# Two of six batches of triangular systems solved by halves of 16 rows and joined by matrix products

## The chip, the cores and the metric

One core of one Trainium2 chip runs the whole program. The metric is the device time of one execution in microseconds (us), the median of several runs. The engines are TensorE (PE, its weight loads shown apart as PEld), VectorE (DVE), ScalarE (ACT), GpSimd (POOL), and SyncE (SP), which issues most of the transfers. They work side by side and wait for each other by semaphores.

## The reference

The program is a recurrent attention over 768 steps for 4 x 8 heads of 40 features, followed by two feed-forward blocks on the 3072 tokens:

```python
for t in range(S):
    y[:, :, t] = np.einsum('bhd,bhde->bhe', rt, state)
    Sa = np.einsum('bhde,bhe->bhd', state, at)
    state_decay = state * wt[:, :, None, :] - np.einsum('bhd,bhe->bhde', Sa, bt)
    state = state_decay + np.einsum('bhd,bhe->bhde', vt, kt)
...
h = np.maximum(np.maximum(x @ w1, x @ w2), x @ w3); x = h @ w_out
h = x @ w_in; sp = np.log1p(np.exp(h)); x = (h * np.tanh(sp)) @ w_out2
```

The steps are cut into chunks of 32. Inside a chunk, the effect of its own steps on each other is a lower triangular system of 32 rows for each head and chunk: with A the products of a and b below the diagonal, the chunk needs the inverse of a unit triangular matrix, which is computed once and then applied by a matrix product.

## The kernel before

**Chunks, units, batches.** The 32 heads go in two groups of 16 through 24 chunks each, so there are 48 chunks, `c` = 0 to 47. Two chunks that follow each other are a unit `n` (24 of them), and four units are a batch `k` (six of them). A unit holds 8 systems in each of four groups of 32 partitions (`zo`); a batch holds 32 "items" in each group, so 128 systems of 32 x 32.

**`pre(n)`** prepares a unit: a scan over the decays (L240), the decayed a, b and k (L244 to L265), and then the `m1` products (L275), which go through a PSUM buffer with the tag `un` that has a single copy. From it ACT copies the triangular part to `ab` (L280), which is one buffer for the whole batch, and VectorE transposes the other part (L282), which GpSimd masks into `ax` (L288).

**`solve(k)`** transposes `ab` so that the 128 systems of the batch lie one in each partition (L303), and eliminates row by row: for s = 0 to 30 a multiply into `tv` (L308) and a subtract from T (L310), both on VectorE, over all rows below s and columns up to s. T then holds the inverse (with sign), is transposed back into `tr[k % 2]` (L314), squared on ACT for a check of its size (L315), and cleared on GpSimd for the next batch (`clear`, L294 and L295).

**`chain(c)`** is the serial work of a chunk in five stages: x0 (L386), its product with the inverse `ups` (L400, weights from `tr`, 16 matmuls of 32 x 32 tiles, four row groups at work), a transpose (L411), the score products (L353, masked at L423), and the output and the next state (L436, L441, L443). `kb` (L325, L329) transposes k and b of the next unit through the same `un` buffer.

**The order.** `start` does units 0 to 3, the solve of batch 0 and the loads of the first chunks. `run` then goes through the chunks in five slots each. A slot issues a stage of the chain; then `fill`, which brings the conversions of the feed-forward weights (L587 to L651) and, from chunk 5 on, eight matmuls of the first feed-forward block (`group`, L661 to L665, L771, L812) a slot; then one step of `pre` for up to three or four units ahead; then some steps of the next solve, spread so that it ends when the chunk that needs it begins; then the rest of the chain's stage; then `kb`, if `un` is not held (`self.held`). The solve of batch 1 can start when units 4 to 7 are prepared, which comes in chunk 4, and must end before chunk 8.

TensorE and VectorE run each of these two blocks (`start`; `run`) in program order, ACT too in `start` and from chunk 4 on. Between the blocks, and on the other engines and queues, a planner puts the instructions in order from simulated times. VectorE's and TensorE's queues are in order, so an instruction that waits holds all that stands behind it.

The second feed-forward block (L941 to L990) runs after the chunks and ends the program.

Of the kernel before, what the change touches and what calls it, by code (L numbers as in the profile page):

```python
# [17 lines left out]
C = 32  # L18
# [74 lines left out]
EARLY = 37  # L93
NPOOL = 14
NE = 3
IN_ORDER = {mybir.EngineType.PE, mybir.EngineType.DVE}


# [55 lines left out]
class Attention:  # L154
# [78 lines left out]
    def pre(self, n):  # L233
# [31 lines left out]
        nc.vector.tensor_tensor(out=bv[:, 8:16], in0=bv[:, 8:16], in1=Qv[:, 8:16], op=ALU.mult)  # L265
        if n >= NB:
            yield
        ps = self.ps_un.tile([128, 2, 4, 64], F32, name="m1", tag="un")
        self.held = True
        for cc in range(2):  # L270
# [10 lines left out]
        akT = p1.tile([128, 4, 2, C], F32, name="akT")  # L281
        nc.vector.transpose(out=akT.rearrange("p j c t -> p c j t"), in_=ps[:, :, :, 0:C])  # L282
        self.held = False
        yield
        for zo in range(4):
            y, g = 1 - zo // 2, zo % 2
# [9 lines left out]

    def solve(self, k):

        nc, p1 = self.nc, self.p1
        abT, T = self.tr[k % 2], self.T  # L300
        if k == 0:
            self.clear()
        nc.vector.transpose(out=abT, in_=self.ab.rearrange("p i s -> p s i"))  # L303
        yield
        for s in range(C - 1):
            n = C - 1 - s
            tv = p1.tile([128, 256], F32, name="tv")[:, 0:n * (s + 1)].rearrange("p (t j) -> p t j", t=n)
            nc.vector.tensor_tensor(out=tv, in0=abT[:, s, s + 1:C].unsqueeze(2).to_broadcast([128, n, s + 1]),  # L308
                                    in1=T[:, s, 0:s + 1].unsqueeze(1).to_broadcast([128, n, s + 1]), op=ALU.mult)
            nc.vector.tensor_tensor(out=T[:, s + 1:C, 0:s + 1], in0=T[:, s + 1:C, 0:s + 1], in1=tv, op=ALU.subtract)  # L310
            yield
        yield

        nc.vector.transpose(out=self.tr[k % 2], in_=T)  # L314
        nc.scalar.activation(out=T, in_=T, func=AF.Square, accum_out=self.gate.le(1e4))  # L315
        if k + 1 < len(self.last):
            self.clear()
        yield
# [144 lines left out]

    def start(self):
        nc, A = self.nc, self.A
        self.under, self.next, self.done, self.held = [], 0, 0, False

        def zeros(*ts):
            for t in ts:
# [45 lines left out]
    def run(self, fill):  # L515
# [6 lines left out]
        for c in range(NC):  # L522
# [4 lines left out]
            for slot in range(5):  # L527
# [12 lines left out]
                if left <= 0 and k + 1 < len(self.last) and self.done > self.last[k + 1] and \  # L540
                        (k == 0 or (c, slot) >= (2 * self.last[k - 1] + 1, 2)):
                    k += 1
                    solve = self.solve(k)
                    left = 34
                    due = 2 * (self.last[k - 1] + 1)
                if left > 0:
                    steps = -(-left // max(1, 5 * (due - c) - slot - 1))
# [725 lines left out]
```

## Time and profile before

| what | us |
|---|---|
| median of 3 runs | 1072.44 |
| lowest and highest run | 1069.83, 1076.19 |
| span of the profiled execution, first to last instruction | 1070.9 |
| TensorE busy | 912.0 (85%) |
| VectorE busy | 878.3 (82%) |
| ScalarE busy | 731.2 (68%) |
| GpSimd busy | 339.6 (32%) |

The profile is of one execution. Its only time of its own is the span, which lies within the spread of the runs; durations below are read from it. Busy shares are means over stages that have different bounds, so the stage in which the change acts has to be looked at by itself. In timelines a group such as x32 is 32 instructions that ran one behind the other and stand in one row, and the time in brackets is how long the engine sat idle before it, with what ended the wait. Matmul instructions overlap each other, so the duration of one is longer than the distance between the starts of two.

### The profile page before, as it was taken

What the parts mean: (1) busy time and instruction counts of PE and PEld (TensorE: products, weight loads), DVE (VectorE), ACT (ScalarE), POOL (GpSimd) and SP (SyncE); (2) the same over time, 40 slices, a digit from 0 to 9 for tenths busy, and PEclk for the clock granted to TensorE, in tenths of its full rate; (3) what the DMA queues carried; (4) which work ended last, traced back from release to release, by engine and by line L of the source; (5) the groups of instructions that cost most, each with busy time, mean ns of one, the idle gap of its engine ahead of it and who ended that gap; (6) DMA issues with size and microseconds to landing.
All of it is one profiled execution on the core that took longest, in us unless ns stands there. A gap on an engine that the chain in (4) does not pass through costs nothing.

```text
span 1070.9 us, 34069 instructions
## 1 busy us (share of the span) xinstructions
PE 912.0 (85%) x14098; PEld 816.2 (76%) x14098; DVE 878.3 (82%) x1698; ACT 731.2 (68%) x1886; POOL 339.6 (32%) x422
## 2 busy tenths in 40 slices
PE   1313456899999999999999999979999999999996
PEld 1212345888888888888998888878889998888995
DVE  7589979978968987886688666899988989898875
ACT  4638864465566665656667777677787887878874
POOL 7437894333233242323114334681201002010000
PEclk9999999999999999999999999999999999999999
DMA  8415532243433434333334443530100000010000
GB/s 211 134 62 159 144 91 64 71 128 84 114 101 100 110 96 113 94 88 97 81 85 104 132 134 90 173 108 5 30 25 31 25 30 26 1 54 1 25 1 28
DMA packets 110615, 87.03 MB, mean 81 GB/s; under 512 B 72740, under 2 KB 89764, under 8 KB 110452
## 3 DMA queue, kind: packets, MB, share of 16 engines
q1 hardware_dynamic: 109712, 84.54, 29.0%
q8 instruction: 113, 1.85, 0.8%
q14 instruction: 50, 0.41, 0.1%
q10 hardware_dynamic: 740, 0.23, 0.1%
HBM read 72.16 MB, written 12.58 MB: 79 GB/s over the span
## 4 chain that ended last, share of the span: by engine, by line
PE 56%; DVE 23%; ACT 9%; issue 4%; DMA 4%; POOL 2%; SPq 0%; ACTq 0%; DVEq 0%; POOLq 0%
PE cops L988 5%; PE cops L989 5%; PE cops L990 5%; PE ys L436 4%; PE bps L661 4%; PE cps L661 4%; PE cps L662 4%; PE cps L663 4%; PE bps L812 3%; DVE T L310 3%; PE bps L662 3%; PE bps L663 3%; DVE tv L308 3%; PE cgps L353 2%; PE cps L665 2%
## 5 line engine op out<-in xcount | busy, mean ns | idle before, releaser
L661 PE MATMUL bps<-bxh,bw 128*128 128x256 f32 x432 | 139.9, 325 | 2.3 <-DVE mx L771 1.4
L662 PE MATMUL bps<-bxl,bw 128*128 128x256 f32 x432 | 124.1, 287 | 3.2 <-DVE bxl L674 3.2
L663 PE MATMUL bps<-bxh,bw 128*128 128x256 f32 x432 | 122.8, 284 | 0.0
L774 POOL TENSOR_TENSOR hl<-mx,hh 128x256 fp32r<-128x256 f32 x72 | 56.7, 787 | 172.8 <-ACT hh L773 145.2
L310 DVE TENSOR_TENSOR T<-T,tv 128x31 f32<-128x31 f32 (+15 forms) x186 | 86.4, 464 | 6.4
L661 PEld LDWEIGHTS bps<-bxh,bw 128*128 128x128 f32 x432 | 82.5, 191 | 11.4 <-DVE mx L771 2.0
L252 POOL TENSOR_TENSOR ax<-ax,pp 40x256 f32<-40x256 f32 x96 | 75.4, 805 | 45.1 <-DMA ax<-in_A_dram 16.1
L662 PEld LDWEIGHTS bps<-bxl,bw 128*128 128x128 f32 x432 | 83.2, 193 | 5.4 <-DVE bxl L674 5.4
L288 POOL TENSOR_SCALAR_AFFINE_SELECT ax<-akT 32x256 f32<-32x256 f32 x96 | 51.3, 535 | 104.6 <-DVE akT L282 100.6
L663 PEld LDWEIGHTS bps<-bxh,bw 128*128 128x128 f32 x432 | 83.1, 192 | 0.0
L972 ACT ACTIVATE e<-e 128x512 f32<-128x512 f32 x93 | 58.6, 630 | 33.3 <-DVE e L970 33.0
L436 PE MATMUL ys<-rs,ls 128*40 128x72 f32 x1536 | 64.8, 241 | 14.6 <-DVE rs L423 9.9
L812 PE MATMUL bps<-hh,bo 128*128 128x256 f32 x360 | 74.9, 291 | 1.5 <-ACT mx L769 1.5
L984 DVE TENSOR_TENSOR gl<-e,gh 128x512 fp32r<-128x512 f32 x93 | 65.8, 708 | 12.5 <-ACT gh L983 12.5
L976 DVE SCALAR_TENSOR_TENSOR e<-e,r 128x512 f32<-128x512 f32 x93 | 66.0, 710 | 11.7 <-ACT r L974 11.4
L275 PE MATMUL m<-bk,ax 40*32 40x64 f32 x1536 | 43.1, 254 | 38.1 <-DMA bk<-in_KB_dram 14.6
L436 PEld LDWEIGHTS ys<-rs,ls 128*40 128x40 f32 x1536 | 55.6, 126 | 22.0 <-DVE rs L423 9.4
L441 DVE TENSOR_TENSOR sv<-ys,pp 40x320 f32<-40x320 f32 x92 | 44.7, 486 | 32.1 <-PE ys L436 31.4
L941 POOL CAST cxh<-cxl 128x1536 fp32r<-128x1536 f32 x5 | 9.1, 1814 | 193.8 <-DMA cxl<-x 193.8
L771 DVE TENSOR_TENSOR mx<-bps,mx 128x256 f32<-128x256 f32 x144 | 60.3, 419 | 11.6 <-ACT mx L769 7.7
L977 DVE SCALAR_TENSOR_TENSOR e<-e,r 128x512 f32<-128x512 f32 x93 | 68.2, 734 | 1.0
L308 DVE TENSOR_TENSOR tv<-tr,T 128x31 f32<-128x31 f32 (+15 forms) x186 | 67.1, 361 | 1.9
(214 smaller groups left out, 3108.3 us busy)
## 6 DMA issues: line engine op xcount, KB each, us to landing
bk<-in_KB_dram SPq DMA_DIRECT2D x24, 448.0 KB
sv<-in_SV_dram SPq DMA_DIRECT2D x96, 80.0 KB
raw<-in_w_dram SPq DMA_DIRECT2D x18, 384.0 KB
w<-in_W_dram SPq DMA_DIRECT2D x21, 231.0 KB
v<-in_VT_dram SPq DMA_DIRECT2D x48, 96.0 KB
rs<-in_RT_dram SPq DMA_DIRECT2D x48, 96.0 KB
cxl<-x SPq DMA_DIRECT2D x12, 384.0 KB
raw<-in_wo_dram SPq DMA_DIRECT2D x13, 320.0 KB
```

The costliest lines, as they stand in the source:

```text
L252: nc.gpsimd.tensor_tensor(out=xv[:, h], in0=xv[:, h], in1=P[ro, h, 0:C], op=ALU.mult)
L308: nc.vector.tensor_tensor(out=tv, in0=abT[:, s, s + 1:C].unsqueeze(2).to_broadcast([128, n, s + 1]), in1=T[:, s, 0:s + 1].unsqueeze(1).to_ ...
L310: nc.vector.tensor_tensor(out=T[:, s + 1:C, 0:s + 1], in0=T[:, s + 1:C, 0:s + 1], in1=tv, op=ALU.subtract)
L436: nc.tensor.matmul(out=self.ys[64 * y:64 * y + 40, p, 0:72], lhsT=l[:, y, p], rhs=r_[:, :, 4 * (p % 4) + 2 * (1 - y) + p // 4], start=True ...
L661: nc.tensor.matmul(out=ps, lhsT=h[:, k], rhs=xh[:, k], start=(k == 0), stop=False)
L662: nc.tensor.matmul(out=ps, lhsT=h[:, k], rhs=xl[:, k], start=False, stop=False)
L663: nc.tensor.matmul(out=ps, lhsT=l[:, k], rhs=xh[:, k], start=False, stop=False)
L771: after(1, lambda ps=ps, mx=mx: nc.vector.tensor_tensor(out=mx, in0=ps, in1=mx, op=ALU.max))
L812: nc.tensor.matmul(out=pss[d][rows], lhsT=lhsT, rhs=rhs, start=first, stop=last)
L976: nc.vector.scalar_tensor_tensor(out=e, in0=e, scalar=1.0, in1=r, op0=ALU.add, op1=ALU.mult)
L977: nc.vector.scalar_tensor_tensor(out=e, in0=e, scalar=-float(np.sqrt(8.0)), in1=r, op0=ALU.add, op1=ALU.mult)
L984: nc.vector.tensor_tensor(out=gl, in0=e, in1=gh.bitcast(F32), op=ALU.subtract)
```

## The change

`HALVED = 2`: batches 0 and 1 are solved by `solve_halves`, the other four as before (`solve_whole` is the old `solve`). The two diagonal blocks of 16 rows of each system are eliminated in the same VectorE operations, 15 steps instead of 31; an access pattern with a step of (C + 1) * H elements covers both. T is then transposed into `tr` as before and, new, also in place. `join` fills the lower left block: a product of `ab` with the second half's inverse (64 matmuls, for 16 items in four row groups), a copy by ACT, a product with the first half's inverse (64 matmuls), and an add by VectorE into `tr`. It runs twice, for items 0 to 15 and 16 to 31, and both times through the `un` buffer. The square for the check reads `tr` and comes behind the joins, and the clearing of T behind that.

Since the join reads `ab` again, `pre` may not write it before: from the start of a halved solve to its second join (`self.joins`), units wait ahead of their `m1` products, and afterwards pass there in their order (`self.turn`). The steps over which `run` spreads the solve are 20 instead of 34 for these batches.

```diff
@@ -265,6 +266,8 @@
         nc.vector.tensor_tensor(out=bv[:, 8:16], in0=bv[:, 8:16], in1=Qv[:, 8:16], op=ALU.mult)
         if n >= NB:
             yield
+        while self.joins or self.turn < n:
+            yield
         ps = self.ps_un.tile([128, 2, 4, 64], F32, name="m1", tag="un")
         self.held = True
         for cc in range(2):
@@ -281,6 +284,7 @@
         akT = p1.tile([128, 4, 2, C], F32, name="akT")
         nc.vector.transpose(out=akT.rearrange("p j c t -> p c j t"), in_=ps[:, :, :, 0:C])
         self.held = False
+        self.turn = n + 1
         yield
         for zo in range(4):
             y, g = 1 - zo // 2, zo % 2
@@ -296,10 +300,73 @@
 
     def solve(self, k):
 
+        if k < HALVED:
+            return self.solve_halves(k)
+        return self.solve_whole(k)
+
+    def join(self, k, h):
+
+        nc, T, tt = self.nc, self.T, self.tr[k % 2].rearrange("p t i -> p i t")
+        ps = self.ps_un.tile([128, 2, 16, 16], F32, name="join", tag="un")
+        items = range(16 * h, 16 * h + 16)
+        for i in items:
+            for zo in range(4):
+                zr = slice(32 * zo, 32 * zo + 32)
+                nc.tensor.matmul(out=ps[zr, 0, i % 16], lhsT=self.ab[zr, i], rhs=tt[zr, i, 16:32], start=True, stop=True)
+        e = self.p1.tile([128, 256], F32, name="tv").rearrange("p (i t) -> p i t", t=16)
+        nc.scalar.copy(out=e, in_=ps[:, 0])
+        yield
+        for i in items:
+            for zo in range(4):
+                zr = slice(32 * zo, 32 * zo + 32)
+                nc.tensor.matmul(out=ps[zr, 1, i % 16], lhsT=T[32 * zo:32 * zo + 16, i], rhs=e[32 * zo:32 * zo + 16, i % 16],
+                                 start=True, stop=True)
+        low = tt[:, 16 * h:16 * h + 16, 16:32]
+        nc.vector.tensor_tensor(out=low, in0=low, in1=ps[:, 1], op=ALU.add)
+
+    def solve_halves(self, k):
+
         nc, p1 = self.nc, self.p1
         abT, T = self.tr[k % 2], self.T
+        H = C // 2
+
+        def halves(x, t, n, j, m):
+            x = x[:, t, j:j + 1]
+            return bass.AP(x.tensor, x.offset, [x.ap[0], [(C + 1) * H, 2], n, m])
+
         if k == 0:
             self.clear()
+        self.joins = True
+        nc.vector.transpose(out=abT, in_=self.ab.rearrange("p i s -> p s i"))
+        yield
+        for s in range(H - 1):
+            n = H - 1 - s
+            tv = p1.tile([128, 256], F32, name="tv")[:, 0:2 * n * (s + 1)].rearrange("p (h t j) -> p h t j", h=2, t=n)
+            nc.vector.tensor_tensor(out=tv, in0=halves(abT, s, [1, n], s + 1, [0, s + 1]),
+                                    in1=halves(T, s, [0, n], 0, [1, s + 1]), op=ALU.mult)
+            to = halves(T, s + 1, [C, n], 0, [1, s + 1])
+            nc.vector.tensor_tensor(out=to, in0=to, in1=tv, op=ALU.subtract)
+            yield
+        nc.vector.transpose(out=self.tr[k % 2], in_=T)
+        tn = T.rearrange("p t j -> p j t")
+        nc.vector.transpose(out=tn, in_=tn)
+        for h in range(2):
+            while self.held:
+                yield
+            self.held = True
+            yield from self.join(k, h)
+            self.held = False
+            self.joins = h == 0
+            yield
+        nc.scalar.activation(out=T, in_=self.tr[k % 2], func=AF.Square, accum_out=self.gate.le(1e4))
+        if k + 1 < len(self.last):
+            self.clear()
+        yield
+
+    def solve_whole(self, k):
+
+        nc, p1 = self.nc, self.p1
+        abT, T = self.tr[k % 2], self.T
         nc.vector.transpose(out=abT, in_=self.ab.rearrange("p i s -> p s i"))
         yield
         for s in range(C - 1):
@@ -463,7 +530,7 @@
 
     def start(self):
         nc, A = self.nc, self.A
-        self.under, self.next, self.done, self.held = [], 0, 0, False
+        self.under, self.next, self.done, self.held, self.joins, self.turn = [], 0, 0, False, False, 0
 
         def zeros(*ts):
             for t in ts:
@@ -541,7 +608,7 @@
                         (k == 0 or (c, slot) >= (2 * self.last[k - 1] + 1, 2)):
                     k += 1
                     solve = self.solve(k)
-                    left = 34
+                    left = 20 if k < HALVED else 34
                     due = 2 * (self.last[k - 1] + 1)
                 if left > 0:
                     steps = -(-left // max(1, 5 * (due - c) - slot - 1))
```

## Rows read from the trace of the kernel before

**Rows 1.** The page: span, and busy tenths of 40 equal slices.
```profile
span 1070.9 us, 34069 instructions
...
PE   1313456899999999999999999979999999999996
...
DVE  7589979978968987886688666899988989898875
```

**Rows 2.** Stretches: length; busy PE, PEld, DVE, ACT, POOL; granted clock; DMA share; GB/s.
```profile
106.00:160.00 54.00, 25.66 (x648) 20.89 (x648) 45.45 (x67) 40.45 (x133) 47.46 (x58) 1.00 0.44 121
...
330.00:690.00 360.00, 346.18 (x7321) 314.17 (x7309) 277.50 (x638) 236.55 (x754) 121.07 (x164) 1.00 0.41 108
```

**Rows 3.** Timeline of VectorE, batch 0's solve: start us, duration us, instruction.
```profile
42.59 0.19 DVE L308 TENSOR_TENSOR tv<-tr,T 128x31 f32<-128x31 f32 x1
...
43.06 0.22 DVE L308 TENSOR_TENSOR tv<-tr,T 128x60 f32<-128x60 f32 x1
...
43.58 0.25 DVE L308 TENSOR_TENSOR tv<-tr,T 128x87 f32<-128x87 f32 x1
...
44.15 0.27 DVE L308 TENSOR_TENSOR tv<-tr,T 128x112 f32<-128x112 f32 x1
...
67.50 1.25 DVE L314 STREAM_TRANSPOSE tr<-T 128x1024 f32<-128x1024 f32 x1
```

**Rows 4.** Timeline of TensorE, small products; in brackets idle before, and releaser.
```profile
23.72 1.92 PE L275 MATMUL m<-bk,ax 40*32 40x64 f32 x60 [0.30 <-DVE bk L265]
...
68.79 0.76 PE L400 MATMUL ups<-X,tr 32*32 32x40 f32 x32 [20.11 <-DVE tr L314]
...
221.12 0.67 PE L400 MATMUL ups<-X,tr 32*32 32x40 f32 x32
221.72 0.39 PE L812 MATMUL bps<-hl,bo 128*128 128x256 f32 x1
```

**Rows 5.** Chain of waits after the solve: start us, us, what.
```profile
68.83 1.16 ACT T L315 x2
...
70.10 1.07 POOL T L294
...
71.56 1.31 POOL t L597
```

**Rows 6.** Groups by line, 0 to 190 us: busy us, mean ns, idle before.
```profile
L303 DVE STREAM_TRANSPOSE tr<-ab 128x1024 f32<-128x1024 f32 x2 | 3.8, 1924 | 0.0
...
L280 ACT COPY ab<-m 128x256 f32<-128x256 f32 x10 | 3.7, 368 | 2.2 <-PE m L275 2.0
...
L443 DVE TENSOR_TENSOR YT<-ys,pp 104x256 f32<-104x256 f32 x5 | 2.1, 426 | 0.2
```

**Rows 7.** Instructions on the tile ups: ns min/median/max, first and last start.
```profile
L400 PE MATMUL ups<-X,tr x1536: 222/223/276, 68.8 to 662.3; 32*32 32x40 f32 x192
```

**Rows 8.** Stretches of batch 1's solve, columns as in rows 2.
```profile
161.20:172.20 11.00, 7.22 (x203) 5.98 (x203) 10.54 (x24) 4.76 (x13) 4.90 (x7) 1.00 0.40 110
172.20:178.00 5.80, 5.39 (x51) 4.75 (x52) 5.59 (x12) 2.48 (x9) 2.35 (x4) 1.00 0.30 58
178.00:187.20 9.20, 4.80 (x148) 4.11 (x147) 8.00 (x17) 4.15 (x11) 3.74 (x5) 0.91 0.05 12
187.20:198.60 11.40, 9.92 (x141) 8.87 (x142) 9.88 (x22) 4.17 (x14) 3.63 (x5) 0.77 0.42 107
198.60:222.00 23.40, 21.43 (x502) 19.13 (x502) 22.18 (x51) 13.97 (x42) 8.05 (x14) 1.00 0.26 65
```

**Rows 9.** Timeline of TensorE, chunk 5.
```profile
187.22 0.96 PE L325 MATMUL kb<-cst,bk 104*128 104x104 f32 x4 [4.42 <-DVE akT L282]
```

**Rows 10.** A stretch behind that gap, columns as in rows 2.
```profile
188.00:190.00 2.00, 2.00 (x34) 1.89 (x32) 1.66 (x4) 1.32 (x5) 1.85 (x4) 0.50 0.43 66
```

**Rows 11.** Chain of waits, one 256-column product behind the gap and later.
```profile
190.77 0.21 PE bps L662
...
201.27 0.12 PE bps L662
```

More of the change, by code (lines that the diff above doesn't have):

```diff
@@ L95 @@
 NE = 3
+HALVED = 2
 IN_ORDER = {mybir.EngineType.PE, mybir.EngineType.DVE}
```

## The prediction

> **What bounds the kernel now.** I read the page's tenths by slice first, then the busy time by stretch, then the timelines of the two stretches in which the first two batches are solved, and the chain that ended last between them. The reader is to see three regimes. Up to about 190 us TensorE is 10 to 70% busy and VectorE, but for one slice, 70% and more [rows 1]. From about 215 us on TensorE is the bound: in the stretch from 330 to 690 us it is busy 346.2 of 360 us, 96%, VectorE 77% [rows 2]. What is won in the first regime moves the start of the second, and what is added to TensorE after it adds to the end. Both edits must be priced so: batch 0 is solved alone, in the first regime; batch 1 is solved during chunks 4 to 7, where one regime passes into the other.
>
> Batch 0: from the first multiply at 42.59 us to the transpose of T at 67.50 VectorE runs nothing but the 62 operations of the solve, and TensorE's first `ups` product waits for that transpose until 68.79 us, having idled 20.1 us [rows 3, 4]. The chain that ended last runs through the same place and on through the clearing of T on GpSimd to the first weight conversion there [rows 5]. So a microsecond saved here is a microsecond of everything behind it.
>
> **Batch 0, part by part.** The distance from one operation's start to the next grows with the elements of one: two of 31 take 42.59 to 43.06, 0.235 us each, two of 87 take 0.285 each [rows 3], so 0.00089 us an element. The halved solve has 15 steps of two operations, of 2(s+1)(15-s) elements: 30, 56, 78, 96, 110, 120, 126, 128 and back. The first seven come to 0.235 + 0.257 + 0.277 + 0.293 + 0.305 + 0.314 + 0.320 = 2.00 us; twice that and 0.32 for the middle one, times two operations, is 8.65 us. The transpose into `tr` stays at 1.25 us [rows 3]; with 0.04 to the next start, 1.29.
>
> New is the in-place transpose of T, with strided input and output. The nearest row is L303, strided input alone, 1.92 us [rows 6]; it can't be under the 1.25 of contiguous data, nor do I see over 2.6 (strided twice). It lies beside the first product of the join, which needs only `tr`, and costs nothing while that product and its copy (below: 2.55 us) last longer.
>
> New are two joins, one behind the other, since each takes the one PSUM buffer `un`. Each is a 64-matmul product, an ACT copy of 256 columns (0.37 us as L280), a second 64-matmul product, and a VectorE add of 256 columns from PSUM (0.43 us as L443) [rows 6]. A float32 matmul is two instructions here: the 16 of `ups` are x32 [rows 4]. So a product is 128. `ups` has the same 32x32 tiles; its 32 instructions take 0.76 us at the start of the kernel and 0.67 later, one lasting 0.26 and 0.22 [rows 4, 7], so a distance of 16 and 14.4 ns. A join's matmul moves 16 columns instead of 40, which can only help, but reads them in steps of 128 bytes. Upper bound: the 60 of L275 in 1.92 us at the start, (1.92 - 0.3)/59 = 27 ns [rows 4]; lower bound, by the columns alone, 16/40 of 16, 6 ns. I take 15 ns (nearest row: the same tile shape). A product is then 1.92 + 0.25 = 2.17 us, a join 2 x 2.17 + 0.37 + 0.43 + four handovers of 0.05 = 5.3, both 10.7 us.
>
> Sum: 8.65 + 1.29 + 10.7 = 20.6 us against 26.2 (42.59 to 68.79): **5.6 us earlier**. Were `ups` of chunk 0, which reads only items of the first half, let in behind the first join and the second's first product, another 3.1 us (5.3 less 2.17) would be won; the order is the planner's, so I keep this as a bound. Bounds for batch 0: from +0.5 (27 ns: 2 x 8.4 + 9.9 - 26.2) to -9. The square and the clearing of T move behind the last join; the first weight conversion on GpSimd stands behind that clearing, 70.10 then 71.56 [rows 5], and moves with it.
>
> **Batch 1.** Removed on VectorE are the same 32 operations and three quarters of the elements. In the trace the stretch from 161 to 222 us has VectorE busy 10.5 of 11.0, 5.6 of 5.8, 8.0 of 9.2, 9.9 of 11.4 and 22.2 of 23.4 us [rows 8]. From 172.2 us (first feed-forward products) to 222 TensorE works 41.5 of 49.8 us, so 8.3 idle; at the later regime's 3.8% it would be 1.9: **6.4 us to win**. Most of it is one gap: 4.4 us before 187.22, in which `kb` waits for VectorE [rows 9], busy 8.0 of 9.2 us there [rows 8], much of it solve steps; of these, one in two is gone. Behind that gap the granted clock is 0.50, so 1.2 of 2.4 GHz, and the same product takes 0.21 us where it takes 0.12 later [rows 10, 11]; the mean of 187.2 to 198.6 is 0.77 [rows 8], so 0.46 of 11.4 us, 5.2, lie at that level, and half of them, **2.6**, goes with the gap. In chunk 4 (161.2 to 172.2), TensorE idles 3.8 us beside a full VectorE; the steps in it shrink by about 2 us: **2.0**.
>
> Against this stand four products, 512 instructions, in chunk 7, where TensorE is 92% busy [rows 8]: 512 x 14.4 ns is 7.4, and each change of shape costs what `ups` costs beyond its own instructions (0.60 us to the next start, 221.12 to 221.72, less 32 x 14.4 ns: 0.14), 0.6: **8.0 us added**. Moved are the `m1` products of units 8 to 11: they write `ab`, which the join reads, so `pre` holds them from the start of solve 1 until its second join, counted out on the code's slots at chunk 7, slot 3; then they follow each other within ten slots, through the same PSUM buffer. Their number is unchanged. What queues behind them: TensorE, in order, waits at each handover for the ACT copy and the VectorE transpose of the one before; a slot's feed-forward matmuls stand between (eight, of which one takes 0.12 to 0.21 us [rows 11], 1 to 1.7 us), so I take **1 us** for all. `kb` is put off by a slot or two and is needed a chunk later. Solve 2 starts three slots later, with most of seven chunks to spare. The waiting of `pre` releases no DMA later: its loads are issued ahead of the wait.
>
> Sum of batch 1: -6.4 - 2.6 - 2.0 + 8.0 + 1.0 = **-2.0 us**.
>
> Total: -5.6 - 2.0 = -7.6 us. The profiled execution's span is 1070.9 us, 1.5 under the median of the runs, and inside their spread; it goes to 1063.3, the median from 1072.4 to 1064.8.
>
> The size that decides is the distance p of the join's instructions: 512 in batch 0's path and 512 in batch 1's, so 1.02 us for each ns. The trace shows tiled products at 14.4 to 16 ns [rows 4, 7]. The Trainium skill speaks against this: "TensorE: Matmul & The Clock Gate", section "Wait — 56ns, not 53.3ns?", has starts of matmuls never closer than about 25 ns, however few columns they move. By it the sum would be some 10 us worse, +3, and the time about 1075. The rows of `ups`, with four row groups at work, don't keep to it, so I go by them.
>
> **Rivals.**
> *Dear joins.* The strided moving operand brings p to L275's 27 ns: batch 0 +0.5, batch 1 8.0 + 6.5 + 1.0 - 11.0 = +4.5, total +5: 1077. It breaks even at 22 ns. For it: this operand is not in the trace. Against: the strided `tr` as weights costs `ups` nothing. By the floor that the Trainium skill states (page and section above) the same mechanism would give 1075.
> *Later bound takes batch 0's gain.* GpSimd is busy 47.5 of 54 us from 106 to 160 [rows 2]; if it, or loads, held the stretch whatever its start, only batch 1's -2 stays: 1070. Against: GpSimd's work is released by VectorE's conversions, so it moves too.
> *More than forecast.* Chunks 4 to 7 fall to the later pace, and `ups` goes in early: some 3 us more from each, -13.6, 1059. For it: both are work that the change takes off VectorE. Against: chunk 7 gets fuller on TensorE.
> *Slower: TensorE stalls at the PSUM buffer.* Chunks 7 to 9 hand `un` over some seven times in order. If two of these waits become like the one before 187.22 (4.4 us and 2.6 of the lower clock each), 14 us come instead of 1: -7.6 + 13 = +5.4; with three, +12: 1078 to 1085, 1080 say. One such wait leaves about -1.6, two decide. For it: VectorE is 95% busy there [rows 8]. Against: that load is what shrinks.
>
> **How the numbers follow.** Forecast 0.47, more than forecast 0.13, dear joins 0.15, gain taken later 0.15, stalls 0.10. Half a per cent, 5.4 us, is about what a measurement of this kernel tells from no change: 1067.0 and 1077.8. Faster is 0.42 of the forecast and the 0.13; slower the stalls and a quarter of the dear joins; the rest is the same. The range goes from 1057 to 1076, leaving out the stalls, part of the dear joins, and a little below. The forecast's own range is 1060 to 1069.
>
> **What would show it.** `ups` of chunk 0 near 63 us (near 60 if let in early); 30 operations in about 8.7 us; a join near 5.3 us; 128 instructions in 2.2 us; no 4 us gap of TensorE in chunk 5; chunk 8 begun some 2 us beyond batch 0's gain, less the joins. Wrong: a join over 7 us, a new gap of TensorE in chunks 7 to 9, or an unmoved start of the feed-forward products.

## The result, and the profile after

The changed kernel takes 1088.05 us, the median of 4 runs (1086.47 to 1090.57), the kernel before 1072.82 in its 4 runs beside them: a ratio of 1.014, with a 95% interval of 1.0114 to 1.0167. It is 1.4% **slower**; the forecast was 1064.8 us, and 1088 lies outside its range. The profiled execution's span is 1084.8 us, 13.9 more than before.

Line numbers below are those of the changed kernel: behind the solve they stand 67 further down (L400 is now L467, L325 now L392, L803 now L870). The two products of a join are L315 and L322, its ACT copy L317 and its VectorE addition L325.

I followed one instruction through both traces: VectorE's copy of `ups` (L402, now L469), which comes once a chunk. Its start in a chunk, less its start in the kernel before, says how far ahead (minus) or behind (plus) the chunk stands. Chunk 0 differs by up to 1.3 us between kernels that are alike up to there, so less than that is not read. The rows of this table are the changed kernel and the experiments told below; the last column is the span's difference. Each row is one profiled execution, which can lie up to 4 us from the median of its kernel ("hold, few products" 4.1 under it, "batch 0, late half" 3.7), so the last columns are to be read with the medians below.

| us against before, start of chunk | 0 | 1 | 4 | 7 | 8 | 9 | 10 | 47 | span |
|---|---|---|---|---|---|---|---|---|---|
| changed kernel | -5.8 | -3.5 | -1.8 | -14.1 | +1.0 | +2.6 | +10.8 | +9.5 | +13.9 |
| batch 0 alone | -6.5 | -4.2 | -2.7 | -3.1 | -3.1 | -3.1 | -3.1 | -1.7 | +0.5 |
| batch 1 alone | -0.7 | -0.5 | -1.2 | -13.4 | +0.6 | +2.2 | +11.1 | +10.3 | +9.6 |
| hold alone | -1.3 | -0.7 | -1.3 | -4.1 | +1.0 | +7.0 | +10.3 | +10.1 | +9.9 |
| no hold | -4.7 | -2.5 | -0.8 | -5.0 | +7.4 | +7.5 | +7.5 | +8.1 | +11.3 |
| hold, few products | -5.1 | -2.8 | -1.4 | -13.4 | -5.4 | -3.9 | +4.9 | +0.4 | -0.3 |
| no hold, few products | -5.4 | -3.1 | -1.8 | -8.7 | -2.1 | -2.1 | -2.1 | -3.8 | -3.3 |
| wide between | -6.9 | -4.6 | -3.2 | -14.5 | +2.0 | +3.5 | +11.8 | +8.5 | +8.4 |
| spread | +0.1 | +0.7 | 0.0 | +8.5 | +19.2 | +19.2 | +19.1 | +17.7 | +17.2 |
| spread, both batches | -7.2 | -4.9 | -3.6 | +5.2 | +15.9 | +16.0 | +16.0 | +13.4 | +16.8 |
| paced | -1.0 | -0.3 | -2.3 | -3.1 | +7.9 | +6.1 | +10.5 | +63.6 | +62.7 |
| batch 0, thirds | -5.9 | -3.5 | -2.1 | -2.0 | -2.0 | -2.0 | -2.0 | -2.0 | -3.2 |
| before, thirds | -0.5 | -0.2 | -0.8 | -1.6 | -1.6 | -1.6 | -1.6 | -1.2 | -3.1 |
| batch 0, late half | -10.3 | -7.0 | -4.6 | -5.0 | -5.1 | -4.9 | -4.9 | -8.0 | -9.0 |
| batch 0, late half, thirds | -10.4 | -7.7 | -5.2 | -5.4 | -5.4 | -5.4 | -5.5 | -7.0 | -8.6 |

In its first row the whole story stands: 5.8 us won at the start, most of it gone by chunk 4; 12.3 more ahead from chunk 4 to 7; then 15.0 lost in chunk 7, 1.6 in chunk 8, 8.2 in chunk 9, and 4.4 at the end.

The timeline of the changed kernel from batch 0's solve to chunk 0's first products answers to [rows 3, 4] (columns as there):

```profile
41.96 0.19 DVE L345 TENSOR_TENSOR tv<-tr,T 128x30 f32<-128x30 f32 x1
...
45.09 0.95 PE L392 MATMUL kb<-cst,bk 104*128 104x104 f32 x4
...
50.62 1.25 DVE L350 STREAM_TRANSPOSE tr<-T 128x1024 f32<-128x1024 f32 x1
51.90 2.06 DVE L352 STREAM_TRANSPOSE T<-T 128x1024 f32<-128x1024 f32 x1
...
52.01 1.90 PE L315 MATMUL join<-tr,ab 32*32 32x16 f32 x128 [3.96 <-ACT ax L540]
...
53.97 0.37 ACT L317 COPY tv<-join 128x256 f32<-128x256 f32 x1 [1.01 <-PE join L315]
...
54.44 0.41 PE L322 MATMUL join<-tv,T 16*32 16x16 f32 x16 [0.53 <-ACT tv L317]
...
56.13 1.69 PE L322 MATMUL join<-tv,T 16*32 16x16 f32 x112 [1.28 <-issue]
57.96 0.59 DVE L325 TENSOR_TENSOR tr<-tr,join 128x256 f32<-128x256 f32 x1 [4.00 <-PE join L322]
58.60 0.41 PE L315 MATMUL join<-tr,ab 32*32 32x16 f32 x16 [0.79 <-DVE tr L325]
...
59.86 1.69 PE L315 MATMUL join<-tr,ab 32*32 32x16 f32 x112 [0.84 <-issue]
...
61.37 0.47 PE L467 MATMUL ups<-X,tr 32*32 32x40 f32 x16
...
63.31 0.49 PE L467 MATMUL ups<-X,tr 32*32 32x40 f32 x16 [1.47 <-issue]
...
63.59 1.68 PE L322 MATMUL join<-tv,T 16*32 16x16 f32 x112
63.88 0.33 DVE L469 COPY ud<-ups 128x160 f32<-128x160 f32 x1 [5.33 <-PE ups L467]
...
66.77 0.41 PE L322 MATMUL join<-tv,T 16*32 16x16 f32 x16 [1.49 <-issue]
```

The reader is to see three things. The 30 operations take 41.96 to 50.62 us, 8.66. A join's 128 instructions take 1.90. And in the middle of a join's product TensorE stops, here for 1.28 us, with "issue" as the reason: it waits for nothing that the profile shows. `ups` was let in between the two products of the second join, and is torn in two by such a stop, 1.47 us.

Two things are easy to overlook. The four stops end at 56.13, 59.86, 63.31 and 66.77 us, and from one to the next TensorE runs 128 matmuls and 128 weight loads: in the trace they end with its 963rd, 1219th, 1475th and 1731st instruction, 256 apart. The seven other kernels below that do both halves of batch 0's join at this place stop at the same four, and the two with the second half later at the first two, where the 1219th is already one of `ups`. So the stops go by the count of instructions, not by the data or the product; no run tests why.

And the clock: in this trace it is recorded only from 176.7 us on (in that of the kernel before from 178.8), so a 1.00 in a stretch ahead of that, as in the first row of [rows 2] and the first two of [rows 8], is no reading. The one run that has it from 107 us on ("no hold, few products") shows 0.50 from 111 to 154 us, and the `kb` at 45.09 us takes 0.95 us, as it does at 0.50 further down (0.96 and 0.95), in place of 0.57 at 1.00: batch 0 runs at the pace of the lower level.

For batch 1, the stretches of the changed kernel (columns as in [rows 2]): chunks 5 and 6, then chunks 7, 8 and 9. They answer to [rows 8]:

```profile
174.66:197.01 22.35, 22.34 (x569) 20.59 (x570) 20.02 (x45) 13.53 (x42) 5.78 (x8) 1.00 0.35 88
```

```profile
197.01:222.84 25.83, 22.22 (x675) 20.01 (x676) 8.24 (x16) 10.78 (x34) 5.20 (x8) 0.67 0.16 39
222.84:237.08 14.24, 13.18 (x379) 11.59 (x380) 6.66 (x15) 5.68 (x18) 5.07 (x11) 1.00 0.43 114
237.08:255.44 18.36, 14.30 (x266) 12.53 (x266) 12.03 (x27) 9.28 (x29) 6.58 (x12) 0.91 0.29 71
```

The kernel before in its chunk 7:

```profile
211.06:221.86 10.80, 9.69 (x215) 8.67 (x216) 10.23 (x21) 8.57 (x26) 4.64 (x8) 1.00 0.30 78
```

In chunks 5 and 6 TensorE is never idle, 22.34 of 22.35 us busy, and the gap of [rows 9] is gone. Then chunk 7 takes 25.8 us in place of 10.8, with a granted clock of 0.67 in the mean. In short stretches of TensorE alone (busy us, granted clock):

```profile
198.00:199.00 1.00, 0.63 (x50) 1.00 0.00 0
199.00:200.00 1.00, 0.41 (x49) 1.00 0.00 0
200.00:201.00 1.00, 0.44 (x51) 0.79 0.05 16
202.00:217.00 15.00, 13.15 (x379) 0.50 0.15 40
```

TensorE was half idle for 3 us, in and behind the first join's second product, and then the clock stands at the lower of its two levels, 1.2 GHz, for some 17 us, though TensorE is now busy 13.15 of 15. Its timeline there:

```profile
198.03 0.59 PE L322 MATMUL join<-tv,T 16*32 16x16 f32 x49
199.59 0.85 PE L322 MATMUL join<-tv,T 16*32 16x16 f32 x79 [0.97 <-issue]
201.23 0.96 PE L392 MATMUL kb<-cst,bk 104*128 104x104 f32 x4 [0.79 <-DVE tr L325]
...
204.25 1.91 PE L315 MATMUL join<-tr,ab 32*32 32x16 f32 x128
...
207.91 0.21 PE L420 MATMUL cgps<-rs,v 40*32 40x32 f32 x1 [1.09 <-issue]
...
210.49 2.15 PE L322 MATMUL join<-tv,T 16*32 16x16 f32 x128
213.40 0.95 PE L392 MATMUL kb<-cst,bk 104*128 104x104 f32 x4 [0.77 <-DVE tr L325]
```

Of the idle 3.6 us of this chunk two are stops (0.97 and 1.09, 512 instructions apart) and two are waits of `kb` for the joins' additions (0.79 and 0.77). Ahead of 198.03 and 210.49 there is no idle time: ACT's two copies are covered.

The held `m1` products arrive from the end of chunk 7 on: units 8 to 11 at 219.0, 223.9, 228.5 and 235.8 us, in place of 162.2, 178.4, 199.8 and 224.0. The timeline of all engines in the changed kernel, at the passage to chunk 9:

```profile
235.76 0.65 PE L278 MATMUL m<-bk,ax 40*32 40x64 f32 x32 [0.88 <-DVE akT L285]
...
241.24 0.37 ACT L283 COPY ab<-m 128x256 f32<-128x256 f32 x1
...
241.70 0.45 DVE L285 STREAM_TRANSPOSE akT<-m 128x256 f32<-128x256 f32 x1 [2.59 <-ACT ab L283]
...
242.21 0.57 PE L392 MATMUL kb<-cst,bk 104*128 104x104 f32 x4 [2.15 <-DVE akT L285]
```

`kb` wants the one buffer `un`; `m1` holds it until ACT, in order, has come to the `ab` copy and VectorE to the transpose. In chunk 9 TensorE is idle 4.1 us, before it was 0.04.

### The profile page after: what moved, and what is told of

It is laid out like the page before. It is cut to its first block, busy times and chain, and to the rows that moved or that the text cites. A ratio compares the mean times of both kernels' runs of the same rounds, so it can differ in the third digit from the quotient of the medians.

```text
span 1084.8 us, 36055 instructions
## 1 busy us (share of the span) xinstructions
PE 931.3 (86%) x15122; PEld 834.7 (77%) x15122; DVE 856.7 (79%) x1640; ACT 733.5 (68%) x1890; POOL 337.0 (31%) x422
## 4 chain that ended last, share of the span: by engine, by line
PE 60%; DVE 17%; ACT 9%; DMA 5%; issue 5%; POOL 2%; SPq 0%; ACTq 0%; DVEq 0%; POOLq 0%
PE cops L1055 5%; PE cops L1056 5%; PE cops L1057 5%; PE bps L879 4%; PE ys L503 4%; PE bps L728 4%; PE cps L728 4%; PE cps L729 4%; PE cps L730 4%; PE bps L729 3%; PE bps L730 3%; PE cgps L420 2%; DMA raw<-in_w_dram 2%; PE m L278 2%; PE cps L732 2%
## 5 line engine op out<-in xcount | busy, mean ns | idle before, releaser
L253 POOL TENSOR_TENSOR ax<-ax,pp 40x256 f32<-40x256 f32 x96 | 74.6, 796 | 52.7 <-DVE pp L241 25.8
L1043 DVE SCALAR_TENSOR_TENSOR e<-e,r 128x512 f32<-128x512 f32 x93 | 66.1, 710 | 11.8 <-ACT r L1041 11.4
L490 DVE TENSOR_TENSOR rs<-cgps,cst 64x256 f32<-64x256 f32 x96 | 40.6, 423 | 43.6 <-PE cgps L420 41.6
L503 PE MATMUL ys<-rs,ls 128*40 128x72 f32 x1536 | 64.7, 242 | 11.8 <-DVE rs L490 6.9
L456 ACT COPY X<-x0ps 128x160 f32<-128x160 f32 x48 | 14.0, 291 | 83.3 <-PE x0ps L453 83.3
L1036 ACT ACTIVATE e<-cps 128x512 f32<-128x512 f32 x93 | 54.9, 590 | 21.0 <-PE cps L732 20.9
```

Source lines behind the costliest of these rows:

```text
L253: nc.gpsimd.tensor_tensor(out=xv[:, h], in0=xv[:, h], in1=P[ro, h, 0:C], op=ALU.mult)
L503: nc.tensor.matmul(out=self.ys[64 * y:64 * y + 40, p, 0:72], lhsT=l[:, y, p], rhs=r_[:, :, 4 * (p % 4) + 2 * (1 - y) + p // 4], start=True ...
L1043: nc.vector.scalar_tensor_tensor(out=e, in0=e, scalar=1.0, in1=r, op0=ALU.add, op1=ALU.mult)
```

## The experiments

Times are medians, beside the kernel before in the same runs; where only a trace is spoken of, the table above has the number.

**Each batch by itself, and the two parts of batch 1.** The first run:

```diff
-HALVED = 2
+HALVED = 1
```

> Batch 0 by halves, batch 1 whole. Theory (the loss is made in chunks 7 to 10, by batch 1's joins and the held m1 products): chunk 4 begins 2 to 3 us earlier than before, nothing is lost later, 1070 us. Rival (what batch 0 wins is absorbed by the weight conversions): chunk 8 begins as before, 1073 us.

1071.56 us, ratio 1.0002 (0.9982 to 1.0022). The 6.5 us at chunk 0 are 3.1 at chunk 10, 1.7 at chunk 47 and nothing at the end.

Second run, batch 1 alone: `HALVED = (1,)`, with `k in HALVED`.

> Batch 0 whole, batch 1 by halves. Theory: chunks 4 to 7 win some 11 us, chunk 7 loses 15 and chunks 9 and 10 lose 10, so about 1088 us, 1 to 3 over the kernel with both. Rival (the early start of batch 0 shifts the weights and makes the loss): under 1080 us.

1083.35 us, ratio 1.013 (1.0108 to 1.0152): the whole loss is batch 1's, though 5 us under the 1088 that was expected.

Third run: both batches solved whole, but the pre steps held from the start of batch 1's solve to its end, which comes at about the same place.

```diff
 def solve_whole(self, k):
+        self.joins = k == 1
...
+        self.joins = False
```

> Both batches whole, as before; only the m1 products of units 8 to 11 wait for the solve of batch 1, as they do in the changed kernel. If the wait makes the step of chunks 9 and 10 and the joins make that of chunk 7: some 10 us over before, 1082 us, with nothing in chunk 7. If the wait makes both: 1090 us or more. If the wait is harmless and all comes from the joins: 1073 us.

1081.85 us, ratio 1.0105 (1.0085 to 1.0124). The hold alone costs 11.6 us between chunks 4 and 10, with not one join in the kernel. But it doesn't keep to chunks 9 and 10, as I had expected: it loses 5.1 us in chunk 7, 6.0 in chunk 8 and 3.3 in chunk 9.

Fourth run: both halved, and the pre steps kept only from the buffer while a join is under way. Later units then put their blocks into `ab` ahead of the joins, which so don't read batch 1's alone.

```diff
-        while self.joins or self.turn < n:
+        while self.joining or self.turn < n:
```

> As the changed kernel, but m1 of units 8 to 11 doesn't wait for the joins (only for the PSUM buffer while a join has it), so batch 1's joins read a buffer ab that partly belongs to batch 2 and its lower left blocks are not those of the reference. If the wait makes the step of chunks 9 and 10: that step goes, that of chunk 7 stays, 1078 us. If the joins make both: 1086 us or more.

1082.21 us, ratio 1.0099 (1.0073 to 1.0126). Chunk 7 still takes 23.2 us, 12.4 more than before, and chunks 8 and 9 now take what they took before. So the joins need no hold to cost their time in chunk 7, and the loss of chunk 9 goes with the hold. The two costs don't add up, though: from chunk 4 to 10 the joins without the hold lose 8.3 us, the hold without joins 11.6, and both together 12.6.

**What of a join costs.** The changed kernel with a sixteenth of batch 1's join products:

```diff
-        for i in items:
+        for i in items if k == 0 else items[0:1]:
```

> Leaves out part of the computation: of the 64 products of each half of batch 1's two joins only the first item's 4 are made, and their result stands for all 16 items; the hold of the pre steps, the two joins' places, their copies and their additions stay. Theory A (the small products themselves, and the granted clock that falls to 0.50 while they are issued, cost the 15 us of chunk 7): the granted clock stays at 1.00 in chunks 7 and 8, chunk 7 takes 11 to 15 us in place of 25.8, the start of chunk 8 stands 8 to 12 us before that of the kernel before, chunks 9 and 10 still lose about 10 us to the held products m1, and the time is 1072 to 1077 us. Theory B (the handovers TensorE to ScalarE to TensorE to VectorE and the single buffer that they hold are the cost): chunk 7 still takes over 20 us and the time is 1081 to 1088 us.

1076.48 us, ratio 1.0033 (1.0012 to 1.0053). The time is theory A's, but chunk 7 takes 18.8 us, between the two, and its granted clock is 0.82, not 1.00: products are a part, handovers another. The same cut without the hold:

> As the run without the hold (both batches halved, the pre steps don't wait for batch 1's joins), but of the products of batch 1's joins only the first item's are made, and their result stands for all 16 items. If the products and the clock at 0.50 are what the joins cost: chunk 7, which took 23.2 us there against 10.8 before, takes 11 to 15 us, and the time is 8 to 12 us below that run's 1082: 1070 to 1074 us. If the handovers through one buffer are: chunk 7 still takes 19 us or more, 1078 to 1082 us.

1068.34 us, ratio 0.9967 (0.9946 to 0.9988), a kernel that does too little work. Chunk 7 takes 17.4 us, again between: of the 12.4 us that the joins cost there, 6.6 come with the handovers alone (3.1 of them more idle TensorE, the rest mostly the clock at 0.80), and the products, with the stops in them, add 5.8. Products without handovers weren't run, so the shares hold in this order. The stretch, in that run, columns as in [rows 2]:

```profile
202.38:219.80 17.42, 13.25 (x243) 11.74 (x244) 8.28 (x18) 9.38 (x29) 5.21 (x8) 0.80 0.22 58
```

and what TensorE waited for in it:

```profile
204.37 0.58 PE L390 MATMUL kb<-cst,bk 104*128 104x104 f32 x4 [1.49 <-DVE tr L325]
...
209.93 0.30 PE L322 MATMUL join<-tv,T 16*32 16x16 f32 x8 [1.55 <-ACT tv L317]
```

The second handover (1.55 us) is idle time although a slot's eight feed-forward products stand in it; with so few products of the join there is less to cover it than in the changed kernel.

**Can the clock be kept up?** The changed kernel, with a product of the whole array behind every fourth item of batch 1's joins:

```diff
+            if k == 1 and i % 4 == 3:
+                self.wide(ps[:, 1])
```

> As the changed kernel, with one product of the whole array (128 by 128 by 256) put after every 4 items of batch 1's join products, 16 in all, whose results nobody reads. Theory A (the clock falls while TensorE issues a long run of 32 by 32 products and little else): the granted clock of 201 to 217 us is 0.9 or more in place of 0.50, the 16 products cost 16 x 0.12 to 0.21 = 2 to 3.4 us, and chunk 7 gets 5 to 8 us shorter: 1080 to 1085 us. Rival (the clock falls because TensorE waits between the products, whatever their shape): the granted clock falls as before and the time is 1089 to 1092 us.

1083.36 us, ratio 1.0102 (1.0062 to 1.0142): theory A's time, but not for its reason. From chunk 7 to 8 it loses 16.5 us, more than the changed kernel's 15.0; what is better is the start (1.1 us, within what starts vary) and the end (4.5 us, told below). TensorE alone, in that run:

```profile
200.00:201.00 1.00, 0.37 (x9) 1.00 0.00 0
201.00:202.00 1.00, 0.93 (x7) 0.73 0.00 0
205.00:208.00 3.00, 2.97 (x164) 1.00 0.00 0
209.00:218.00 9.00, 8.32 (x173) 0.50 0.19 56
```

The clock fell again right behind a wait (0.70 us), came back among the products of the second join's first half, and fell once more. That small products as such bring it down doesn't hold: in the changed kernel, too, the first 128 (195.0 to 196.5) run at 1.00.

**Spread instead of bunched.** The join in 8 parts of 4 items, one to a slot, its two halves on both sides of the slot's chain stage; the lower-left blocks copied aside, so nothing is held. Batch 0 whole.

```diff
+        nc.scalar.copy(out=self.abl[:, 0:32], in_=self.ab[:, :, 0:C // 2])
...
-        for h in range(2):
+        for h in range(8):
```

> Batch 0 is solved whole, as in the kernel before. Batch 1 is halved, its join is cut into 8 of 4 items, one to a slot between the products of the feed-forward block, and the lower-left blocks are copied aside by ScalarE at the start, so that no pre step waits. If the change's cost lies in where its joins stand and in the hold, and not in the products as such: the granted clock stays at 1.00, 256 products at 15 ns are 3.9 us and 8 handovers of 0.3 to 0.8 us are 2.4 to 6.4 us against the 12 us that VectorE's relief won in chunks 4 to 7; the start of chunk 10 stands 2 to 6 us before that of the kernel before and the time is 1065 to 1069 us. Rival (halving batch 1 is dear wherever the joins stand, since small products let the clock fall and every handover costs over 1 us): the start of chunk 10 stands 4 to 10 us after, 1075 to 1081 us.

> As the run with the spread joins, with batch 0 halved as in the changed kernel too. If batch 0's gain adds (2.7 us at chunk 4 where batch 0 alone was halved) and the tail does not take it back: 2 to 4 us below the run with the spread joins, 1062 to 1067 us. If the tail takes it back again (about 3 us, as in the run with batch 0 alone): the same as the run with the spread joins, within 1 us.

1090.16 us, ratio 1.0154 (1.0119 to 1.0188), and with batch 0 halved 1090.01 (1.0152). The rival, and worse: 8.5 us lost before chunk 7, 10.6 in it, with a granted clock of 0.70 in chunk 5 and 0.83 in chunk 6. TensorE waits in chunk 5:

```profile
185.61 0.96 PE L397 MATMUL kb<-cst,bk 104*128 104x104 f32 x4 [3.56 <-DVE akT L286]
...
195.11 0.62 PE L324 MATMUL join<-tv,T 16*32 16x16 f32 x32 [1.58 <-DVE T L355]
```

Finer parts bring more handovers, and the solve's steps, two a slot, still crowd VectorE; but this edit changes three things at once, so which of them its 19 us come from isn't shown.

**Is it the close succession of the held steps?** The hold alone, but with six slots at least between one unit's `m1` and the next.

```diff
-        while self.joins or self.turn < n:
+        while self.joins or self.turn < n or self.tick < self.free:
```

> As the run with the hold alone (both batches solved whole, the pre steps held as in the changed kernel), but once let go a pre step's products m1 follow those of the pre step before by six slots or more. If the close succession of the held steps is the cost: the 14 us between the starts of chunks 7 and 10 fall to 6 or less, and the time is 1073 to 1077 us against 1081.9 for the hold alone. If the delay as such is (what hangs on the late pre steps comes late however they are spaced): 1080 to 1086 us.

1136.92 us, ratio 1.0623 (1.0583 to 1.0663). The loss grows from 10.5 us at chunk 10 to 63.6 at chunk 47. But the pace binds every unit from unit 4 on, not only the held ones: the `m1` of unit 7, which batch 1's solve needs, comes at 183.1 us in place of 152.1, and that of unit 12 three chunks late. So this run doesn't answer its question, and how much of the hold's cost is succession and how much is delay stays open.

**Where does batch 0's gain go?** At the passage to the second feed-forward block, batch 0 alone has this (timeline, all engines):

```profile
718.26 3.86 POOL L1009 TENSOR_TENSOR cxl<-cxl,cxh 128x1536 fp32r<-128x1536 f32 x1
...
718.76 3.91 DVE L1044 SCALAR_TENSOR_TENSOR ce<-ce,spare 128x512 f32<-128x512 f32 x1
...
722.70 0.43 DVE L870 TENSOR_TENSOR mx<-bps,mx 64x256 f32<-64x256 f32 x1
...
723.18 0.64 PE L1055 MATMUL cops<-c_ax,gh 128*128 128x320 f32 x1 [4.98 <-DVE mx L870]
```

and the kernel before, with the same order of instructions on VectorE:

```profile
717.88 1.88 POOL L941 CAST cxh<-cxl 128x1536 fp32r<-128x1536 f32 x1 [0.93 <-DMA cxl<-x]
...
721.04 0.43 DVE L803 TENSOR_TENSOR mx<-bps,mx 64x256 f32<-64x256 f32 x1
...
721.23 3.48 POOL L942 TENSOR_TENSOR cxl<-cxl,cxh 128x1536 fp32r<-128x1536 f32 x1
...
721.52 0.41 PE L988 MATMUL cops<-c_ax,gh 128*128 128x320 f32 x1 [1.55 <-DVE mx L803]
```

An operation of VectorE that is 0.85 us long before (the mean of L977 on `ce`) ends only 0.55 us after GpSimd's subtraction beside it has ended. Before, GpSimd waited 0.93 us for a load, and the subtraction fell behind the maximum that TensorE wants; with batch 0 halved it doesn't wait, and the subtraction falls ahead of it. The Trainium skill says that VectorE and GpSimd share one pair of ports, which the instruction that starts first has to itself until it ends, and that a VectorE operation with two SBUF inputs asks for it when the GpSimd operation reads SBUF, as both do here ("SBUF — State Buffer", section "SBUF: two separate sides"); the trace agrees, 3.91 us beside 3.86. The other traces bear it out: this operation takes 3.91 us in four kernels of the table (changed, batch 0 alone, no hold, spread with both batches), and these four lose 2.2 to 4.4 us from chunk 47 to the end; the other eleven lose 0.5 at most. The test cuts the subtraction in three:

```diff
-            self.nc.gpsimd.tensor_tensor(out=lo, ...)
+            for k in range(3):
+                self.nc.gpsimd.tensor_tensor(out=lo[:, k], ...)
```

> Batch 0 alone halved, and GpSimd's subtraction that splits x in the second feed-forward block cut into three of 512 columns each (1.3 us in place of 3.86). If batch 0's gain is lost at the passage to that block because VectorE's long operation there (3.91 us) runs as long as GpSimd's beside it and stands ahead of the maximum that TensorE waits for: the wait of 4.98 us falls below 3 us, the end follows chunk 47 as in the kernel before, and the time is 2 to 3.5 us below that of batch 0 alone: about 1068 to 1069 us against 1071 for the kernel before. Rival (the loss has another cause, such as the order of the conversions): as batch 0 alone, within 0.1% of the kernel before.

> The kernel before with the same cut of GpSimd's subtraction alone. In its trace VectorE's 2.90 us operation stands behind the maximum, so the cut is worth less than 1 us there: 1070 to 1072 us. If it gains 2 us or more, the cut is worth that by itself and says nothing of batch 0.

Batch 0 alone: 1068.73 us, ratio 0.9965 (0.995 to 0.9981), and the wait is 2.83 us:

```profile
718.46 1.75 DVE L1045 SCALAR_TENSOR_TENSOR ce<-ce,spare 128x512 f32<-128x512 f32 x1
...
720.24 0.43 DVE L870 TENSOR_TENSOR mx<-bps,mx 64x256 f32<-64x256 f32 x1
...
720.73 0.63 PE L1056 MATMUL cops<-c_ax,gh 128*128 128x320 f32 x1 [2.83 <-DVE mx L870]
```

But the kernel before with the cut takes 1070.21, ratio 0.9976 (0.9958 to 0.9993), 2.8 us less, though its wait at this place is not shorter (1.75 us). By what was written beforehand the cut is then worth something by itself, and the time alone says nothing of batch 0; the shorter wait, 4.98 to 2.83, does, and the four kernels above.

**The second half of batch 0's join.** In the changed kernel its first product stands ahead of chunk 0's `ups`, and the rest between `ups` and the transpose. Items 16 to 31 are first read in chunk 4, so it can go behind chunk 0's state:

```diff
-        finish(solve)
+        for _ in range(16):
+            next(solve)
+        self.second = solve
...
+                if (c, slot) == (0, 4):
+                    finish(self.second)
```

> Batch 0 alone halved, and the second half of its join (items 16 to 31, wanted from chunk 4 on) put into chunk 0 behind the products of its state, in place of ahead of chunk 0's second product. If the second half's 7 us between chunk 0's first product and its transpose take back batch 0's gain: the start of chunk 1 stands 5 to 7 us before that of the kernel before in place of 4.2, and that of chunk 4 4 to 6 in place of 2.7. Rival (VectorE's work in chunks 0 to 3 bounds them): chunk 4's stands 2 to 3.5 us before, as without the delay, and the time is that of batch 0 alone, 1071 us; with the first theory it is 1067 to 1070 us.

> Both edits on batch 0 alone: the late second half and the subtraction in thirds. If both theories hold: 4 to 6 us below the kernel before, 1065 to 1067 us. If only the passage to the second block mattered: 1068 to 1069 us. If neither: 1071 us.

1067.29 us, ratio 0.9945 (0.9928 to 0.9962), and with the thirds 1065.75, ratio 0.994 (0.9918 to 0.9963); the two intervals don't tell the thirds' share here. Both kernels do all of the reference's work and beat the kernel before. The first theory holds: 7.0 us at chunk 1, 4.6 at chunk 4. TensorE in chunk 0 of the first:

```profile
51.57 1.91 PE L315 MATMUL join<-tr,ab 32*32 32x16 f32 x128 [3.74 <-DVE tr L350]
...
57.31 0.49 PE L467 MATMUL ups<-X,tr 32*32 32x40 f32 x16 [0.78 <-DVE tr L325]
...
58.84 0.49 PE L467 MATMUL ups<-X,tr 32*32 32x40 f32 x16 [1.04 <-issue]
...
68.30 1.91 PE L315 MATMUL join<-tr,ab 32*32 32x16 f32 x128
```

Why it stands 3 us further ahead at chunk 47 than at chunk 10 wasn't tested; the execution that was profiled is the fastest of its ten, 3.7 us under their median.

## Why the prediction was wrong

**Batch 0, the start: right in its sum.** Forecast 5.6 us earlier; `ups`' copy starts 5.8 earlier, of which 0.6 stood already at the solve's first multiply (41.96 against 42.59). Operation by operation: 30 operations 8.65 us, measured 8.66; a product 2.17, measured 1.90 and 0.06 to the copy; the in-place transpose 1.25 to 2.6, measured 2.06 and hidden beside that product; the addition 0.43, measured 0.59. The distance p of the join's instructions, on which the rival of the dear joins hung, is (1.90 - 0.21)/127 = 13 ns, from 0.21 us for one. The 25 ns of the Trainium skill ("TensorE: Matmul & The Clock Gate", section "Wait — 56ns, not 53.3ns?") don't hold for these tiled products. Of the working's two values from `ups`, 16 ns was read at 68.79 us, at the lower pace, and 14.4 at 1.00. What the working lacked were the stops called "issue": 1.28 and 0.84 us in the joins up to `ups`, 1.47 in `ups`. Letting `ups` in early, worth 3.1 us in the working and left out of its sum, only paid for them: that the sum came out is luck.

**Batch 0, the end: the rival of the later bound, half.** "So a microsecond saved here is a microsecond of everything behind it" failed. Of 6.5 us (batch 0 alone) 2.7 are left at chunk 4. One cause is shown: the second half of the join stood in chunk 0's own path; moved behind it, 4.6 are left. But that kernel's own 10.3 at chunk 0 shrink by 5.7, where batch 0 alone loses 3.8, so something else in chunks 0 to 4 takes back part of what is won. The chain that ended last points at the loads of feed-forward weights (`raw`): between 65 and 120 us it goes through one of them before (3.36 us at 116.06), and through three with batch 0 alone (3.17 us at 65.54, 4.18 at 80.81, 3.16 at 112.58). No run moved these loads, so loads, GpSimd and VectorE aren't parted. The rest is lost 650 us later, where the kernel, 1.7 us ahead at chunk 47, has GpSimd's subtraction under VectorE's operation. The changed kernel loses 4.4 us at its end, and there too one of this operation's three takes 3.91 us, their mean 1.90 in place of 0.85.

**Batch 1.** Its forecast was -2.0 us, and the table gives +12.6 (from -1.8 at chunk 4 to +10.8 at chunk 10). Three runs part this in steps:

- Handovers without products and hold: -1.8 to -2.1, so -0.3. In it the relief of VectorE is 6.9 us (to chunk 7), and chunk 7 gives back 6.6. The forecast had 11.0 of relief (6.4 + 2.6 + 2.0), and 1.0 for all waits.
- Products added (no hold): -0.8 to +7.5, so +8.3, 8.6 more. Forecast 8.0: close, but not for its reasons, since 5.8 of it is chunk 7, with the stops and the clock in it, and the rest relief that doesn't come.
- Hold added (the changed kernel): +12.6, 4.3 more. By itself it costs 11.6; some of the 12.3 us that chunks 4 to 7 seemed to win is pre work put off.

Against the forecast these are 4.1 us of relief that didn't come, 5.6 more for the handovers, 0.6 more for the products and 4.3 for the hold: the 14.6 between -2.0 and +12.6.

So the step that failed is the sentence on what queues behind the moved `m1` products: "I take **1 us** for all". It is the only term for waits in the sum of batch 1; the handovers of its joins have none. The handovers measured 6.6 us and the hold 4 to 12. The term counted on a slot's eight feed-forward matmuls, 1 to 1.7 us, to cover each handover. Without the joins' products a handover is up to 1.6 us of idle TensorE even with those between, the five waits of batch 1's joins 4.5 us together; in the changed kernel's chunk 7 the copies are covered and the additions leave 1.6 us, but the stops, which the working lacked, add 2.1. Behind such idle time the granted clock fell to 0.50, which the working gave only as a gain (2.6 us at [rows 9, 10]). The gain came: chunks 5 and 6 run at 1.00. But 17 us at 0.50 came in its place, two chunks later. The relief of 11.0 us is the second term that failed, by 4.1; why it fell short isn't shown. In chunk 7 the 15.0 us are, worked out: 5.5 for the four stretches of join products in it, 2.5 more of idle TensorE (3.6 against 1.1), and some 4.5 for the half clock (13.15 us busy at 0.50, less the 4.1 of joins in them, already counted; half of the 9 that are left). The 2.5 that are left are work which this chunk didn't have before: an `m1` of 64 instructions (1.2), a second `kb` (0.5) and seven more feed-forward matmuls (0.8).

**The rivals.** "Slower: TensorE stalls at the PSUM buffer", with 0.10, is nearest to what happened in chunks 7 and 9; its waits are shorter than the 4.4 us that I gave each, but there are more of them, and stops besides. Dear joins fell by their mechanism: p is 13 ns, not 27. But with the stops three products in a row of batch 0 took 1.90, 3.38 and 2.95 us, 21 ns an instruction in the mean, about half way to that rival's price. "Would show it": the 30 operations and the missing gap in chunk 5 came as written; `ups` was let in early, and its halves came at 61.4 and 63.3 us, not near 60; chunk 8 began 1.0 us late in place of 2 us beyond batch 0's gain; a join took 6.5 us (52.0 to 58.55), under the 7 that were to count against it. The sign of "wrong" that came true is the new gaps in chunks 7 to 9.

## What to carry to other kernels

Work moved from an engine with in-order neighbours to another costs its handovers too: count each as the idle time of the waiting engine, with the clock that it may bring down behind it, and don't count on neighbouring work to cover it unless a row shows such a handover covered. A wait that guards a buffer puts off a whole stage, and what chunks seem to win meanwhile is partly work owed. Split a join by who needs it when: the half that is wanted four chunks later paid only once it was out of the first chunk's path; and look for a gain's loss far behind, where a shift of 2 us changes which instructions of two engines meet.

## What the runs showed of the hardware

- TensorE stops inside runs of small tiled products, with nothing in the profile that it waits for: 1.28, 0.84, 1.49 and 0.97 us in the joins of the changed kernel, 1.47 in its first `ups`. From one to the next lie 256 instructions, or a multiple of it to within one (weight loads counted). What it is wasn't tested.
- A join's product of 128 instructions took 1.48 us in chunk 6 at a granted clock of 1.00, 1.91 and 2.15 in chunk 7 at 0.50, and 1.90 in batch 0, where the clock isn't recorded and `kb` takes as long as at 0.50 (0.95 us, 0.57 at 1.00).
- An in-place transpose of 32 x 32 blocks with strided input and output takes 2.06 us against 1.25 for contiguous data and 1.92 with strided input alone [rows 3, 6].
